# Retention and a gated feed-forward layer on one core: two transposes moved to TensorE, and other block widths behind the first 512 tokens

## The chip, the core and the metric

The kernel runs on one core of a Trainium2 chip. A core has a matrix engine (TensorE, PE in the profile), a vector engine (VectorE, DVE), a scalar engine (ScalarE, ACT), a general engine (GpSimd, POOL) and a sync engine (SyncE, SP), which here only issues transfers (DMAs). TensorE writes into PSUM, which VectorE and ScalarE read; everything else lies in SBUF. The metric is the device time of one execution in microseconds, as the median of several runs. Before the change it is 331.77 us over 8 runs (331.12 to 333.21).

## The reference

Eight batches of eight heads, 576 positions, head size 64. The first half is retention, a causal linear attention with a decay per head:

```python
scores = scale * np.matmul(q, k.transpose(0, 1, 3, 2))
gamma = 1.0 - 2.0 ** (-5.0 - np.arange(H, dtype=np.float32))
rel = pos[:, None] - pos[None, :]
Dmat = np.where(rel >= 0, gamma[:, None, None] ** rel[None, :, :], 0.0)
attn_out = np.matmul(scores * Dmat[None, :, :, :], v)
```

Its result is laid out as x with 4608 rows (tokens) of 512 columns, and the second half is a feed-forward layer with 1536 hidden columns:

```python
gate = 1.0 / (1.0 + np.exp(-(x @ w_gate)))
out = (gate * (x @ w_val)) @ w_out
```

## The kernel before, in words

The kernel works in bf16 with sums in float32. The decay is split into a factor on q and a factor on k, so that the scores only need a triangular mask.

**Attention.** The first 768 tokens (three pairs of 128-token chunks) are done in a start phase of their own. The rest are 30 steps, numbered 0 to 29 (`STEPS`), of 128 tokens and all heads each; step s fills columns 768 + 128 s of the transposed activations `xT` (the last two swapped). A step needs its q, k and v loaded (three transfers of 256 KB, `load`, L118), q and k scaled and cast to bf16 (`cast_qk`, L283, into `natural_qk`), v cast (L288), and a transposed copy `T` of q and k. The copy is made by `cross` (L290 to L294): one transposing DMA from SBUF to SBUF, issued by SP. `casts_to` (L590) puts loads, casts and transpose of a step into the program together, three steps ahead of the step's slot; steps 0 and 1 are put in before the blocks begin. SP takes everything in program order: the loads of step s+1 stand in front of the transpose of step s. GpSimd does most casts, also in program order; VectorE casts q of steps 0 and 1 and v of step 0.

On TensorE a step is a *slot* (`slot`, L511): the values of the step before (`intra` L493 with the masked scores, `inter` L507 with the running state), then the scores of this step (`scores`, L469, from `T`) and its state products (`products`, L477). VectorE then masks the scores (L484). The *after-phases* 0, 1 and 2 of a slot take the values out of PSUM: ScalarE casts one half of a value tile into `xT` (L526) and copies the shares that belong to the other tile (L529), VectorE adds the shares to the other half (L537), adds the state (L546, L550, L552), and ScalarE or GpSimd casts the state to bf16 (L446). The value tiles have one PSUM bank each (`VALS`: pools `pv_psum` and `tr_psum`), so the values of the next slot need all of these reads done. The score tiles have two banks (`qk_psum`).

**Feed-forward.** It goes by blocks of tokens. The first block, 512 tokens, is part of the start phase; its end is `op_first` (L888), with four output tiles stored by VectorE and ScalarE (L928 to L934). Behind it `BLOCKS` (L937) lists blocks of 256, 256, four of 384 and four of 512 columns. For each of the 12 chunks of hidden columns a block does four matmuls for the gate and four for the value (L625), a sigmoid on ScalarE and a product on VectorE. With 256 columns or fewer, gate and value share a PSUM bank and one unit of eight matmuls (L633 to L641); wider ones use a bank and a piece of four matmuls for each (L647 to L654). The banks of the units come from `ffn_psum`, which has three. Then come the output matmuls (`op_units`, L692), 12 for each 128 tokens, with a copy to SBUF on ScalarE (L668) and a store.

**The order.** Nothing is scheduled by a planner; the program order is what each engine runs. The loop over `BLOCKS` interleaves the two halves: `order` (L579) lists the phases ("slot", "after0", "after1", "after2" of each step), `end` is the last phase that the next block needs (the after-phases of the slot behind its last step), and after each unit or piece `advance` runs as many of the block's phases as its share of columns calls for:

```python
advance(begin + min(todo, -(-todo * max(0, gone - wait) // (total - wait - 3 * 2048))))
```

`gone` counts columns of matmul work done, `total` those of the block; 3 x 2048 columns at the end are left free. `wait`, 2048 columns, is set only for the block at token 512, so that slot 0 comes after its second unit.

Of the kernel before, what the change touches and what calls it, by code (L numbers as in the profile page):

```python
# [10 lines left out]
BF16 = mybir.dt.bfloat16  # L11
# [5 lines left out]
def kernel(  # L17
# [19 lines left out]
    nc = tc.nc  # L37

    B, H, S, D = q.shape
    NT, DM = out.shape  # L40
    DFF = moe_w_gate.shape[1]
    P = 128
    M = H // 2
# [7 lines left out]
    att_pool = ctx.enter_context(tc.tile_pool(name="att", bufs=3))  # L51
# [152 lines left out]
    ident = consts.tile([P, P], BF16)  # L204
# [41 lines left out]
    on_pool, on_act, on_dve = nc.gpsimd.tensor_copy, nc.scalar.copy, nc.vector.tensor_copy  # L246
# [8 lines left out]
    turned = {}  # L255
# [16 lines left out]
    natural_qk = {}  # L272
# [5 lines left out]
    def cast_qk(s, i, eng):  # L278
        c = STEPS[s][1]
        if i == 1:  # L280
            natural_qk[s] = nat_pool.tile([P, 2, M, P], BF16, tag="qk", name=f"qk_{s}")
        tab = (qtab, ktab)[i][:, c, :].rearrange("p (y m) -> p y m", y=2).unsqueeze(3).to_broadcast([P, 2, M, D])
        eng.tensor_tensor(out=natural_qk[s][:, i].rearrange("p m (y d) -> p y m d", y=2),  # L283
                          in0=by_halves(loaded[s][1 - i]), in1=tab, op=ALU.mult)

    def cast_v(s, eng):
        natural["v", s] = nat_pool.tile([P, H, D], BF16, tag="v", name=f"v_{s}")
        eng(out=natural["v", s], in_=loaded[s][2])  # L288

    def cross(s):  # L290
        t = att_pool.tile([P, 2, M, P], BF16, tag="T", name=f"T_{s}", bufs=5)
        nc.sync.dma_start_transpose(out=t.rearrange("p j m t -> p (j m) t"),
                                    in_=natural_qk[s].rearrange("p j m d -> p (j m d)"))
        turned[s] = t  # L294

    turned = {}
# [133 lines left out]
    def pair_out(A, a, *engs):  # L430
        t0 = (2 * A + a) * P
        k = M // len(engs)
        for i, eng in enumerate(engs):
            eng(out=xT[:, i * k:(i + 1) * k, t0:t0 + P], in_=pair_ps[2 * A + a][i * k][0])

    running = {}
    totals = {}

# [5 lines left out]
    def keep_state(key, src, eng):  # L444
        state[key] = new_state(key)
        eng(out=state[key], in_=src)  # L446
# [8 lines left out]
    VALS = [(pv_psum, "pv"), (tr_psum, "tr")]  # L455
# [55 lines left out]
    def slot(s):  # L511

        if s > 0:
            intra(s - 1)
            inter(s - 1)
        if s < NS:
            scores(s)
            if STEPS[s][1] < LAST:
                products(s)
        if s < NS:  # L520
            mask(s)
# [33 lines left out]
    def after(s, i):  # L555

        makes = s < NS and STEPS[s][1] < LAST
        to_bf16 = on_act if s < 6 else on_pool
        if i > 0 and s > 0:
            leave_other(s - 1, i - 1)  # L560
        if i < 2 and s > 0:
            leave_own(s - 1, i)
        if i < 2 and makes:
            add_state(s, i)
        if i > 0 and makes and (s, i - 1) in totals:
            b, c = STEPS[s]
            keep_state((b, c, i - 1), totals.pop((s, i - 1)), to_bf16)


    def first_batch_state():  # L570

        whole = new_state((0, LAST - 1, NJ - 1))
        for hh in range(2):
            for y in range(2):
                (nc.vector.tensor_copy if hh == y else nc.sync.dma_start)(
                    out=whole[half(y), hh::2, :], in_=sbd[3][half(hh), 2 * y:2 * y + 2, half(hh)])
        state[0, LAST - 1, NJ - 1] = whole

    order = []  # L579
    for s in range(NS + 1):  # L580
        order += [("slot", s), ("after0", s), ("after1", s), ("after2", s)]

    done = {"ld": 0, "cast": 0}

    def loads_to(s):
        while done["ld"] <= min(NS - 1, s):
            load(done["ld"])
            done["ld"] += 1

    def casts_to(s):  # L590
        while done["cast"] <= min(NS - 1, s):
            x = done["cast"]
            loads_to(x + (1 if x < 12 else 2))
            cast_qk(x, 1, nc.gpsimd)
            cast_qk(x, 0, nc.vector if x < 2 else nc.gpsimd)
            cross(x)
            cast_v(x, on_dve if x == 0 else on_pool)
            done["cast"] += 1

    def run_phase(kind, s):  # L600
        if kind == "slot":
            slot(s)
            if s == 3:
                first_batch_state()
            casts_to(s + LEAD_CAST)
        else:
            after(s, int(kind[5]))

# [51 lines left out]
    def leave():  # L660
        r, ob = stores.pop(0)
        for p0, r0, w in rows(r, P):
            nc.sync.dma_start(out[r0:r0 + w, :], ob[p0:p0 + w])

    def store(opp, r0, eng=None):

        ob = osb_pool.tile([P, DM], FP32, tag="osb", name=f"ob_{r0}")
        (eng or on_act)(out=ob, in_=opp)  # L668
        stores.append((r0, ob))
        if len(stores) > KEEP:  # L670
            leave()
# [27 lines left out]
    def ffn_units(t0, n):  # L699
        gvs = {}  # L700
        yield from h_units(gvs, range(NFC), t0, 0, n)
        yield from op_units(gvs, t0, n)
# [3 lines left out]
    def advance(end):  # L706
        nonlocal at
        while at < end:
            run_phase(*order[at])
            at += 1  # L710

    def upto(s):

        return order.index(("after2", s + 1)) + 1

    def last_step(t1):
        return max(s for s in range(NS) if at_col[s] < t1)
# [170 lines left out]
    def op_first(fcs, nbs, opps):  # L888
        for fc in fcs:
            for nb in nbs:  # L890
                nc.tensor.matmul(opps[nb], lhsT=gvs[fc][:, nb * P:(nb + 1) * P], rhs=wo_sb[:, fc, :],  # L891
                                 start=(fc == 0), stop=(fc == NFC - 1))
# [23 lines left out]
    keep_state((1, 0, 1), st_tiles[1], on_act)  # L916
    op_first((5, 6, 7, 8, 9), range(3), opps)
    casts_to(0)
    third_intra([PV, QK[0]])
    pair_st(2, 1)  # L920
# [4 lines left out]
    nc.vector.tensor_copy(out=running[1], in_=st_tiles[1])  # L925
    keep_state((1, 1, 1), running[1], on_act)
    op_first((10, 11), range(3), opps)
    store(opps[0], 0, on_dve)  # L928
    opps.append(qk_psum.tile([P, 512], FP32, tag="qk", name="op_0_3"))
    op_first(range(0, 6), (3,), opps)  # L930
# [2 lines left out]
    store(opps[2], 2 * P, on_dve)  # L933
    store(opps[3], 3 * P, on_act)  # L934
    casts_to(1)

    BLOCKS = [(512, 256), (768, 256)] + [(t, 384) for t in range(1024, 2560, 384)]  # L937
    BLOCKS += [(t, 512) for t in range(2560, NT, 512)]
    pieces = 0
    for w, (t0, n) in enumerate(BLOCKS):  # L940
        nxt = BLOCKS[w + 1] if w + 1 < len(BLOCKS) else None
        end = upto(last_step(nxt[0] + nxt[1])) if nxt else len(order)
        todo = end - at
        begin = at
        total = 2 * NFC * 4 * n + 12 * 512 * (n // P)
        gone = 0
        wait = 2048 if t0 == 512 else 0
        for cols in ffn_units(t0, n):
            gone += cols
            pieces += 1  # L950
            if stores and (nxt is None or w + 2 == len(BLOCKS) and pieces % 4 == 0):
                leave()
            advance(begin + min(todo, -(-todo * max(0, gone - wait) // (total - wait - 3 * 2048))))
        advance(end)
    while stores:
        leave()
# [29 lines left out]
```

## Time and profile before

| | |
|---|---|
| median of 8 runs | 331.77 us (331.12 to 333.21) |
| profiled execution, its own time | 331.83 us |
| its span in the profile | 330.1 us |
| granted TensorE clock | 1.00 of full speed |
| TensorE matmul / weight load busy | 321.1 / 181.0 us |
| VectorE / ScalarE / GpSimd busy | 154.4 / 131.1 / 117.0 us |
| block at token 512 | 52.59 to 72.04 us |
| block at token 768 | 72.04 to 90.29 us |
| from there to the block at token 2560 | 90.29 to about 193.6 us |
| transposing DMAs (`T`) | 30, median 4.7 us from issue to landing (3.0 to 6.3) |
| loads of k, q, v (256 KB each) | 26 of each, median 4.7, 5.2 and 5.5 us to landing |

The page gives the busy time of each engine, and then the costliest groups of instructions: line, engine, operation, tiles, how many, busy time and mean of one, and the idle time ahead of them with what ended it. Matmuls overlap in the pipeline, so a matmul's own duration is longer than the distance from one to the next, and it is the distance that counts. The timeline has one row for a run of equal instructions: start, duration, engine, line, operation, count, and in brackets the idle time before it and its releaser. The chain of waits is the work that ended last, followed back from the end.

### The profile page before, as it was taken

The page shows a single profiled execution, that of the slowest core. Times are in us where ns is not written, and L with a number is a line of the kernel's source. Part 1 is how long each engine was busy: PE and PEld are TensorE (multiplying, and loading weights), DVE is VectorE, ACT ScalarE, POOL GpSimd, SP SyncE. Part 2 cuts the span into 40 slices and gives each one's busy share as a digit, 9 for nine tenths or more (in the row PEclk, how much of TensorE's full clock was granted, in tenths as well). Part 3 has the DMA queues.
Part 4 walks back from the last instruction along what each step waited for, and adds up shares of the span by engine and source line. Part 5 has one row for each costly group of instructions (what it writes and reads, how often), then busy time and mean ns, then how long its engine had stood idle before and what let it go on. Part 6 is the DMA issues. An engine that isn't in the chain of part 4 may idle for free.

```text
span 330.1 us, 9167 instructions
## 1 busy us (share of the span) xinstructions
PE 321.1 (97%) x3749; PEld 181.0 (55%) x3776; DVE 154.4 (47%) x367; ACT 131.1 (40%) x332; POOL 117.0 (35%) x171
## 2 busy tenths in 40 slices
PE   8899999899999999999999999999999999999996
PEld 8764546758566456456556544444444444444443
DVE  5845536637446255246346625541555056204310
ACT  6655544445443244243343433432443233333321
POOL 5674543445364636115534536052444000000000
PEclk9999999999999999999999999999999999999999
DMA  8999999999999999996796998859314900020003
GB/s 220 306 363 352 339 278 198 188 189 165 196 203 177 178 243 177 236 222 133 202 149 129 204 239 175 122 143 211 65 32 115 326 11 0 3 95 32 2 33 95
DMA packets 146906, 55.68 MB, mean 169 GB/s; under 512 B 127280, under 2 KB 138800, under 8 KB 146864
## 3 DMA queue, kind: packets, MB, share of 16 engines
q1 hardware_dynamic: 146720, 54.97, 81.2%
q8 instruction: 29, 0.48, 0.6%
q10 hardware_dynamic: 144, 0.13, 0.1%
q14 instruction: 13, 0.11, 0.1%
HBM read 37.75 MB, written 9.44 MB: 143 GB/s over the span
## 4 chain that ended last, share of the span: by engine, by line
PE 79%; DMA 14%; SPq 4%; POOL 2%; issue 1%; ACT 0%
PE h L625 48%; PE op L692 24%; PE val L493 2%; SPq L130 2%; DMA wv<-in_moe_w_val_dram 2%; DMA k<-in_k_dram 2%; DMA T<-qk 2%; DMA k32p<-in_k_dram 2%; DMA v32p<-in_v_dram 2%; DMA v<-in_v_dram 2%; DMA wo<-in_moe_w_out_dram 2%; DMA wg<-in_moe_w_gate_dram 1%; PE row L477 1%; PE row L469 1%; PE val L507 1%
## 5 line engine op out<-in xcount | busy, mean ns | idle before, releaser
L625 PE MATMUL h<-xT,wv_sb 128*128 128x384 bf16 (+2 forms) x470 | 102.4, 336 | 0.5
L625 PE MATMUL h<-xT,wg_sb 128*128 128x384 bf16 (+2 forms) x479 | 102.8, 337 | 0.1
L653 DVE TENSOR_TENSOR gv<-g,h 128x384 bf16<-128x384 bf16 (+1 forms) x96 | 59.6, 621 | 61.1 <-PE h L625 54.1
L649 ACT ACTIVATE g<-h 128x384 bf16<-128x384 f32 (+1 forms) x96 | 52.2, 544 | 89.1 <-PE h L625 85.8
L692 PE MATMUL op<-wo_sb,gv 128*128 128x512 bf16 x361 | 81.3, 379 | 1.0 <-issue 0.6
L625 PEld LDWEIGHTS <-wg_sb 128*128 128x128 bf16 x480 | 46.2, 98 | 36.9
L625 PEld LDWEIGHTS <-wv_sb 128*128 128x128 bf16 x480 | 45.5, 98 | 33.6
L692 PEld LDWEIGHTS <-gv 128*128 128x128 bf16 x372 | 36.0, 98 | 42.3
L446 POOL CAST sb<-s 128x256 bf16<-128x256 f32 x35 | 14.0, 403 | 101.1 <-DVE s L550 66.3
L484 DVE TENSOR_TENSOR pt<-row,tri 128x256 bf16<-128x256 f32 x60 | 22.6, 419 | 53.1 <-PE row L477 47.3
L668 ACT COPY ob<-op 128x512 f32<-128x512 f32 x33 | 19.3, 586 | 61.8 <-PE op L692 58.3
L283 POOL TENSOR_TENSOR qk<-k,ktab 128x512 bf16<-128x512 f32 x30 | 31.3, 1044 | 25.4 <-DMA k<-in_k_dram 21.0
L283 POOL TENSOR_TENSOR qk<-q,qtab 128x512 bf16<-128x512 f32 x28 | 29.2, 1044 | 3.1 <-DMA q<-in_q_dram 2.4
L288 POOL CAST v<-v 128x512 bf16<-128x512 f32 x29 | 17.7, 612 | 9.2 <-DMA v<-in_v_dram 7.8
L537 DVE TENSOR_TENSOR xT<-val,share 128x128 bf16<-128x128 f32 x54 | 15.4, 285 | 11.7 <-ACT share L529 11.6
L529 ACT COPY share<-val 128x128 f32<-128x128 f32 x54 | 15.1, 280 | 5.6 <-DVE xT L537 4.7
L526 ACT CAST xT<-val 128x128 bf16<-128x128 f32 x60 | 15.6, 264 | 1.4 <-PE val L507 1.4
L550 DVE TENSOR_TENSOR s<-s,row 128x256 f32<-128x256 f32 x39 | 16.1, 412 | 0.0
L641 DVE TENSOR_TENSOR gv<-g,h 128x256 bf16<-128x256 bf16 x24 | 10.1, 420 | 12.6 <-ACT g L639 12.0
L639 ACT ACTIVATE g<-h 128x256 bf16<-128x256 f32 x24 | 9.1, 386 | 12.5 <-PE h L625 12.0
L493 PEld LDWEIGHTS <-v 64*64 64x64 bf16 x480 | 6.5, 107 | 11.5 <-issue 11.3
L891 PE MATMUL op<-wo_sb,gv 128*128 128x512 bf16 x45 | 11.2, 379 | 0.3 <-issue 0.2
(96 smaller groups left out, 243.3 us busy)
## 6 DMA issues: line engine op xcount, KB each, us to landing
out_dram<-ob SPq DMA_DIRECT2D x31, 256.0 KB, 2.4
k<-in_k_dram SPq DMA_DIRECT2D x26, 256.0 KB, 4.7
q<-in_q_dram SPq DMA_DIRECT2D x26, 256.0 KB, 5.2
v<-in_v_dram SPq DMA_DIRECT2D x26, 256.0 KB, 5.5
wg<-in_moe_w_gate_dram SPq DMA_DIRECT2D x12, 256.0 KB, 5.4
wv<-in_moe_w_val_dram SPq DMA_DIRECT2D x12, 256.0 KB, 5.3
wo<-in_moe_w_out_dram SPq DMA_DIRECT2D x12, 256.0 KB, 5.3
k32p<-in_k_dram SPq DMA_DIRECT2D x6, 256.0 KB, 5.6
```

What stands on the lines that cost most here:

```text
L283: eng.tensor_tensor(out=natural_qk[s][:, i].rearrange("p m (y d) -> p y m d", y=2), in0=by_halves(loaded[s][1 - i]), in1=tab, op=ALU.mult)
L288: eng(out=natural["v", s], in_=loaded[s][2])
L484: nc.vector.tensor_tensor(out=probs[s][:, y], in0=row_ps[s][y][:, 0], in1=tri.unsqueeze(1).to_broadcast([P, M, 64]), op=ALU.mult)
L526: nc.scalar.copy(out=xT[:, own, cols_of(s, j)], in_=val_ps[s][j][:, own])
L529: nc.scalar.copy(out=shares[s, j], in_=val_ps[s][1 - j][:, M:M + 2])
L537: nc.vector.tensor_tensor(out=xT[:, other, cols_of(s, j)], in0=val_ps[s][j][:, other], in1=shares.pop((s, j)), op=ALU.add)
L550: nc.vector.tensor_tensor(out=new, in0=running[b], in1=p, op=ALU.add)
L625: nc.tensor.matmul(out, lhsT=w_sb[:, kc, fc * P:(fc + 1) * P], rhs=xT[:, kc, t0 + a:t0 + e], start=(kc == 0), stop=(kc == NKC - 1))
L649: nc.scalar.activation(out=g[:, 0:n], in_=h1[:, 0:n], func=AF.Sigmoid)
L653: nc.vector.tensor_tensor(out=gvs[some[0]][:, a:e], in0=g[:, 0:n], in1=h2[:, 0:n], op=ALU.mult)
L668: (eng or on_act)(out=ob, in_=opp)
L692: nc.tensor.matmul(opp, lhsT=gvs[fc][:, nb * P:(nb + 1) * P], rhs=wo_sb[:, fc, :], start=(fc == 0), stop=(fc == NFC - 1))
```

## The change

A function `turn_step` makes the transposed copy of a step on TensorE: 8 transposes (a matmul with the identity) into the two banks of the value tiles, four in each, one bank copied out by ScalarE and one by VectorE. Steps 0 and 1 use it in place of the transposing DMA (`TURNED = 2`). Step 0 is turned between two groups of output matmuls of the first block; step 1 gets a phase of its own in `order`, between after-phases 1 and 2 of slot 0. The blocks behind the first 512 tokens become 256, 384, 384 and six of 512 columns, so ten blocks become nine, and which phases fall into which block changes with them. `wait` goes.

```diff
+    TURNED = 2
+
+    def turn_step(s):
+
+        t = att_pool.tile([P, 2, M, P], BF16, tag="T", name=f"T_{s}", bufs=5)
+        for i, ((pool, tag), eng) in enumerate(zip(VALS, (on_act, on_dve))):
+            ps = pool.tile([P, M, P], BF16, tag=tag, name=f"turn_{s}_{i}")
+            for m in range(M):
+                nc.tensor.matmul(ps[:, m, :], lhsT=natural_qk[s][:, i, m, :], rhs=ident, is_transpose=True,
+                                 start=(m == 0), stop=(m == M - 1))
+            eng(out=t[:, i], in_=ps)
+        turned[s] = t
...
-        order += [("slot", s), ("after0", s), ("after1", s), ("after2", s)]
+        order += [("slot", s), ("after0", s), ("after1", s)] + [("turn", s + 1)] * (s + 1 == 1) + [("after2", s)]
...
-            cross(x)
+            if x >= TURNED:
+                cross(x)
...
+        elif kind == "turn":
+            turn_step(s)
...
     op_first((10, 11), range(3), opps)
+    turn_step(0)
     store(opps[0], 0, on_dve)
...
-    BLOCKS = [(512, 256), (768, 256)] + [(t, 384) for t in range(1024, 2560, 384)]
-    BLOCKS += [(t, 512) for t in range(2560, NT, 512)]
+    BLOCKS = [(512, 256), (768, 384), (1152, 384)] + [(t, 512) for t in range(1536, NT, 512)]
...
-        wait = 2048 if t0 == 512 else 0
...
-            advance(begin + min(todo, -(-todo * max(0, gone - wait) // (total - wait - 3 * 2048))))
+            advance(begin + min(todo, -(-todo * gone // (total - 3 * 2048))))
```

In the changed kernel the lines behind `pair_out` stand 13 to 16 lines lower, so that L537 becomes L550 and L625 becomes L641.

## The prediction

> **What bounds the kernel now.** I read the page first, then the tensor engine's waits, then the timeline around its longest wait, then the chain of waits from 45 to 80 us. The page's busy times, and its shares of the chain that ended last:
>
> ```profile
> PE 321.1 (97%) x3749; PEld 181.0 (55%) x3776; DVE 154.4 (47%) x367; ACT 131.1 (40%) x332; POOL 117.0 (35%) x171
> ...
> PE 79%; DMA 14%; SPq 4%; POOL 2%; issue 1%; ACT 0%
> ```
>
> TensorE is busy 321.1 of 330.1 us. From 90.3 us on, the timeline shows attention slots and FFN pieces back to back, so only TensorE work counts there. What can be won lies between 50 and 85 us, where these waits are:
>
> ```profile
> PE val L493 <- DVE xT L537: 0.8, 1, 0.8
> ...
> PE row L469 <- DMA T<-qk: 0.3, 1, 0.3
> ```
>
> The longest one on TensorE's timeline (start, us, what):
>
> ```profile
> 63.45 0.60 PE L625 MATMUL h<-xT,wv_sb 128*128 128x256 bf16 x4
> 63.98 0.22 PE L493 MATMUL val<-pt,v 64*64 64x64 bf16 x2
> 65.04 0.31 PE L493 MATMUL val<-pt,v 64*64 64x64 bf16 x14 [0.84 <-DVE xT L537]
> 65.16 0.32 PE L507 MATMUL val<-T,sb 64*64 64x64 bf16 x16
> 65.60 0.32 PE L469 MATMUL row<-T 64*64 64x64 bf16 x16
> 65.75 0.30 PE L477 MATMUL row<-v,qk 64*64 64x64 bf16 x16
> 65.98 0.61 PE L625 MATMUL h<-xT,wg_sb 128*128 128x256 bf16 x4
> ```
>
> This is slot 2. It starts its values for step 1 and must wait until VectorE has taken step 0's values out of the same PSUM bank. Why VectorE is late is in ScalarE's and VectorE's own timelines:
>
> ```profile
> 62.40 0.38 ACT L639 ACTIVATE g<-h 128x256 bf16<-128x256 f32 x1 [0.49 <-PE h L625]
> 62.68 0.26 ACT L526 CAST xT<-val 128x128 bf16<-128x128 f32 x1
> 63.47 0.27 ACT L529 COPY share<-val 128x128 f32<-128x128 f32 x1 [0.53 <-DVE xT L537]
> 63.64 0.41 ACT L446 CAST sb<-s 128x256 bf16<-128x256 f32 x1
> 63.94 0.66 ACT L639 ACTIVATE g<-h 128x256 bf16<-128x256 f32 x2
> ```
>
> ```profile
> 63.16 0.28 DVE L537 TENSOR_TENSOR xT<-val,share 128x128 bf16<-128x128 f32 x1
> 63.36 0.41 DVE L546 TENSOR_TENSOR sf<-s,row 128x256 bf16<-128x256 f32 x1
> 64.36 0.42 DVE L641 TENSOR_TENSOR gv<-g,h 128x256 bf16<-128x256 bf16 x1 [0.60 <-ACT g L639]
> 64.70 0.28 DVE L537 TENSOR_TENSOR xT<-val,share 128x128 bf16<-128x128 f32 x1
> ```
>
> ScalarE's share (63.47) waits for VectorE's first xT; the next sigmoid, whose matmuls ended near 63.0, starts at 63.94; VectorE's product waits for it, and the second xT, which TensorE needs, stands behind that product. The transposed tile is not far off either:
>
> ```profile
> 59.23 6.33 DMA T<-qk
> 65.60 0.32 PE row L469 x16
> ```
>
> T_2 lands at 65.56, some 0.1 us after the rows could have started.
>
> **What the skill says.** "TensorE: Matmul & The Clock Gate", section "Architectural detail", has ScalarE and VectorE strictly first in, first out; the trace agrees, the sigmoid above stayed behind the share. "PSUM — Partial Sum Buffer", section on bank collisions, says that the two engines must be kept apart on one bank even for reads; the trace agrees, shares waited 4.7 us for xT, 8 times. The TensorE page's "Back-to-back issue gap" gives N/2.4 + 2.5 ns for N columns; pieces of four follow here at 0.437, 0.650 and 0.864 us, which is 109.3, 162.5 and 215.9 ns a matmul, so it holds. Its "Part 4: PE-mode transpose" gives about 275 ns for a transpose in a kernel; the trace has four in a row (39.00 to 39.23 us) costing 0.23 us, so I use 57 ns.
>
> **The change, part by part.**
>
> *Blocks.* 10 blocks become 9, so 96 matmuls and weight loads of h go while their columns stay. Columns 512 to 2560 before: 192 at 109.3 + 384 at 162.5 = 83.39 us. After: 96 at 109.3 + 192 at 162.5 + 192 at 215.9 = 83.15 us. Gain 0.24 us. Weight loads (98 ns) fit under even the 109 ns matmul.
>
> *Transposes on TensorE.* Two turns of 8 transposes, 16 x 57 ns = 0.92 us, all on TensorE's busy path, plus about 0.06 us because turn 0's second half needs the bank that VectorE's copy L403 leaves at 50.44: cost 0.97. Each turn also adds a ScalarE copy (0.59 to 0.74 us, row L320) and a VectorE copy (none from bf16 PSUM is in the trace; between 0.42 us, a half-size copy, and 0.69, a PSUM copy of this shape; I take 0.68). For turn 0 they go ahead of the stores of the first 512 rows: ScalarE then ends the store of op_0_3 near 53.95, just when slot 0 needs that bank. For turn 1 they run from about 57.0 to 58.0, before slot 1 at 58.4. I count both at nothing; if that cover fails, each costs up to 0.6. The buffers of T_0 and T_1 come free to T_5 and T_6 only after these copies and slots 1 and 2, long before those transposes are issued (77.9 and 83.5 before).
>
> *Transposes off SP and DMA.* Two issues leave SP (2.94 and 2.43 us). Slot 0 waited for T_0: it took 0.79 us (54.34 to 55.13) where I put a free one at 0.5, gain 0.3. Slot 1 took 0.87 against 0.75 for a free full slot (later ones take 0.69 to 0.79): gain 0.12. T_2 comes earlier: from 54.7 (T_0) to 76.9 (T_4, k_6 lands one load later) four steps took 5.55 us each; at about 1.2 us a load (k_2 landed 55.96, one load after T_0) a transpose is worth some 1.9 us, two of them 3.8. T_2 so lands near 61.7 and T_3 near 67.3, estimates good to about 1 us.
>
> *Order of attention in block 512.* This decides. The next block is now 384 wide, so 17 phases (slots 0 to 3, their after-phases, the turn) instead of 12 go into the 512-token block, and the initial wait of 2048 columns is gone. After unit i (12 h units, 2048 columns each) the count reached is 17*2048*i/30720 rounded up (36864 columns of the block less 3 x 2048): 2, 3, 4, 5, 6, 7, 8, 10, 11, 12, 13, 14. So slot 0 comes after unit 1, turn 1 after 3, slot 1 after 5, and after unit 8 both the last after-phase of slot 1 and slot 2: nothing lies between them. Before, one unit lay between (units 10 and 11). Slot 3 follows unit 12, its predecessor's last phase unit 11.
>
> Follow it with 0.875 us a unit, from 53.1 (52.59 + 0.5): unit 5 ends 58.43, slot 1 59.18, units 6, 7, 8 end 60.05, 60.93, 61.80. A sigmoid starts 0.25 after its unit and takes 0.38; a product follows and takes 0.42. Sigmoid 7 61.18, product 7 61.60, first xT ends 62.22, share to 62.52, the state cast to 62.83, so sigmoid 8 starts at 62.72 (engines overlap by some 0.1), product 8 63.14, second xT ends 63.76, TensorE resumes at 63.82. With the 0.94 us from resumption to the next piece, as before, slot 2 ends at 64.76, against 62.55 if free: 2.2 us lost. Before it lost 2.09 - 0.75 = 1.34. Loss +0.86. T_2's rows come about 64.2, so T_2 is in time.
>
> The same walk for slot 3: unit 12 ends 68.26, the second xT ends 69.34, the slot ends 70.34, 1.33 lost (as slot 2 before, same spacing). Before, slot 3 stood behind the output matmuls and took 0.69, nothing lost. Loss +1.33. T_3's rows come near 69.8, about 2.5 us after my estimate. SP and GpSimd keep their order past slot 3; its two small state DMAs and 0.77 us of VectorE copies now fall into the output stage, where VectorE idled from 69 to 73.6.
>
> *Blocks behind.* Slots 4 and 5 took 0.95 and 0.93 us among 256-column units. In 384-column pieces they have two pieces behind the last after-phase, as slots 7 to 18 of before, which show no such wait: gain 0.4. Slots 7 to 14 come up to 6 us earlier; supply of 5.6 us a step stays ahead of their 6 to 7.5.
>
> *Sum:* -0.24 + 0.97 - 0.30 - 0.12 + 0.86 + 1.33 - 0.40 = +2.1 us on a span of 330.1. The profiled execution's time is 331.83, 1.7 above its span, and the median is 331.77; the same margin gives 333.9.
>
> **Rivals.**
>
> *The transposes are late (12%).* T_3 now is needed near 69.8 instead of 73.3. For: T landed up to 6.3 us after issue, with DMA share 1.2 to 1.5 from 50 to 75 us. Against: two transposes fewer. If loads ahead of it keep today's pace (T_3 at 71.7 before: k_5, one load behind it, lands at 72.9), it holds slot 3 by about 1.9 more: 335.8. It decides from a landing after 69.8.
>
> *The waits are hidden, faster (13%).* If xT of slot 1 and 2 leaves PSUM before slots 2 and 3 arrive, their losses are 0 and before's 1.34 is won too: +0.97 - 0.24 - 0.3 - 0.12 - 1.34 - 0.4 = -1.4, so 330.4. For: the wait is only 2 to 3 short operations. Against: product 8 cannot start before unit 8 has ended, which alone (0.25 + 0.38 + 0.42 + 0.28) holds slot 2 for 1.3 us. It decides if TensorE resumes there within 0.3 us.
>
> *About a wash (9%).* The chain is short at both places (1.3 at slot 2, 0.5 at slot 3, including the slower restart): 2.1 - 0.9 - 0.8 = +0.4, 332.2. It would need ScalarE to take each sigmoid as soon as its unit ends.
>
> **Numbers.** My case has 66%, with its own range 332.8 to 335.0 (slot 2 losing only 1.3 + 0.2 of restart, or both copies uncovered). The 8-in-10 range takes in the wash and nearly all of late T_3, not the faster case: 331.3 to 335.8. This kernel can tell 0.2%, 0.66 us, from no change. Slower: 66 + 12 + 1 (the upper edge of the wash) = 79%; same 8%; faster 13%.
>
> **What would show it.** Slot 2 and slot 3 each with an idle of TensorE put down to VectorE's xT (now L550), about 1.9 and 1.1 us; no wait for T at slots 0 to 3; T_2 landing 61 to 63; four transposes at 0.23 us; 864 h matmuls in L641; the block of 768 starting near 75.5. I am wrong if TensorE runs through slot 2, or if a wait for T or for ScalarE's stores appears before 70 us.

## The result and the profile after

The changed kernel takes 335.06 us (median of 11 runs, 333.73 to 337.2), the kernel before 331.77 us beside it (median of 32): a ratio of 1.010, 95% interval 1.0074 to 1.0126. It is slower, as forecast, by 3.3 us where 2.1 were forecast. The profiled execution took 334.12 us over a span of 332.4 us, which is 2.3 us more than before's and 0.2 us above the forecast sum. Of the 11 and the profiled one, seven ran at a granted clock of 1.000 and took 333.73 to 335.06 us (median 334.12), five at 0.990 to 0.995 and took 335.82 to 337.2, so the median holds about another microsecond that the trace does not show.

The same rows of the page as before, the busy times and the shares of the chain that ended last:

```profile
PE 321.1 (97%) x3664; PEld 172.3 (52%) x3696; DVE 155.4 (47%) x357; ACT 130.4 (39%) x322; POOL 117.2 (35%) x171
...
PE 82%; DMA 10%; SPq 4%; issue 1%; DVE 1%; ACT 1%; POOL 0%; ACTq 0%
```

TensorE's busy time is the same 321.1 us. It has 80 weight loads fewer: 96 of h are gone, as the same columns go in fewer instructions, and the 16 transposes are new. By this page, on which the ends of matmuls are modelled, the 2.3 us are idle time of TensorE. VectorE and ScalarE have entered the last chain with 1% each. The waits of TensorE that are new or larger (total us, times, longest):

```profile
PE val L506 <- DVE xT L550: 1.9, 2, 1.0
...
PE val L506 <- ACT share L542: 0.6, 1, 0.6
...
PE turn L444 <- DVE apart L403: 0.2, 1, 0.2
```

The wait for a transposed tile, 0.3 us before, is gone. On TensorE's timeline (start, us, what) slots 2 and 3 look like this:

```profile
61.69 0.60 PE L641 MATMUL h<-xT,wv_sb 128*128 128x256 bf16 x4
62.90 0.22 PE L506 MATMUL val<-pt,v 64*64 64x64 bf16 x2 [0.61 <-ACT share L542]
64.15 0.31 PE L506 MATMUL val<-pt,v 64*64 64x64 bf16 x14 [1.03 <-DVE xT L550]
...
64.80 0.61 PE L641 MATMUL h<-xT,wg_sb 128*128 128x256 bf16 x4
...
68.40 0.22 PE L506 MATMUL val<-pt,v 64*64 64x64 bf16 x2
69.46 0.31 PE L506 MATMUL val<-pt,v 64*64 64x64 bf16 x14 [0.84 <-DVE xT L550]
...
70.06 5.35 PE L708 MATMUL op<-wo_sb,gv 128*128 128x512 bf16 x23
```

Slot 2 goes from the end of the unit at 62.13 to 64.80: 2.67 us where it took 2.09. Slot 3 goes from 68.31 to 70.06: 1.75 us where it took 0.69. ScalarE's and VectorE's timelines in front of slot 2's resumption:

```profile
61.51 0.38 ACT L655 ACTIVATE g<-h 128x256 bf16<-128x256 f32 x1 [0.16 <-PE h L641]
...
62.59 0.27 ACT L542 COPY share<-val 128x128 f32<-128x128 f32 x1 [0.53 <-DVE xT L550]
62.75 0.41 ACT L459 CAST sb<-s 128x256 bf16<-128x256 f32 x1
63.05 0.39 ACT L655 ACTIVATE g<-h 128x256 bf16<-128x256 f32 x1
```

```profile
62.27 0.28 DVE L550 TENSOR_TENSOR xT<-val,share 128x128 bf16<-128x128 f32 x1
62.47 0.41 DVE L559 TENSOR_TENSOR sf<-s,row 128x256 bf16<-128x256 f32 x1
63.48 0.42 DVE L657 TENSOR_TENSOR gv<-g,h 128x256 bf16<-128x256 bf16 x1 [0.59 <-ACT g L655]
63.81 0.28 DVE L550 TENSOR_TENSOR xT<-val,share 128x128 bf16<-128x128 f32 x1
```

It is the walk of the prediction, piece by piece: share behind the first xT, state cast, sigmoid 8 at 63.05, product 8 at 63.48, second xT at 63.81, TensorE at 64.15. Each piece comes 0.3 us later than in the walk, as the block began at 53.41 and not at 53.1. One wait more than forecast is seen: TensorE's first two value matmuls stood 0.61 us for ScalarE's share, an earlier link of the same chain. The last part of the chain of waits is:

```profile
62.75 0.41 ACT sb L459
63.16 0.29 ACT g L655
...
63.48 0.42 DVE gv L657
63.90 0.21 DVE xT L550
...
64.15 0.31 PE val L506 x14
```

The other place is the first turn. Its second half waits for VectorE's copy out of the bank:

```profile
50.01 0.39 PE L444 MATMUL turn<-ident,qk 128*128 128x128 bf16 x4
50.60 0.38 PE L444 MATMUL turn<-ident,qk 128*128 128x128 bf16 x4 [0.21 <-DVE apart L403]
50.83 2.75 PE L907 MATMUL op<-wo_sb,gv 128*128 128x512 bf16 x12
```

From 50.01 to 50.83 are 0.82 us for 8 transposes, and by as much block 512 starts later (53.41 after 52.59). The second turn, beside h units, costs 0.44.

### The profile page after: what moved, and what is told of

Its sections match the earlier page's. It is cut to its first block, busy times and chain, and to the rows that moved or that the text cites. A ratio compares the mean times of both kernels' runs of the same rounds, so it can differ in the third digit from the quotient of the medians.

```text
span 332.4 us, 8969 instructions
## 1 busy us (share of the span) xinstructions
PE 321.1 (97%) x3664; PEld 172.3 (52%) x3696; DVE 155.4 (47%) x357; ACT 130.4 (39%) x322; POOL 117.2 (35%) x171
## 4 chain that ended last, share of the span: by engine, by line
PE 82%; DMA 10%; SPq 4%; issue 1%; DVE 1%; ACT 1%; POOL 0%; ACTq 0%
PE h L641 50%; PE op L708 24%; DMA wv<-in_moe_w_val_dram 3%; SPq L130 3%; PE val L506 2%; DMA v<-in_v_dram 2%; DMA wg<-in_moe_w_gate_dram 2%; DMA k32p<-in_k_dram 2%; PE row L490 1%; PE row L482 1%; DMA wo<-in_moe_w_out_dram 1%; PE val L520 1%; PE op L697 1%; PE op L907 1%; SPq L142 1%
## 5 line engine op out<-in xcount | busy, mean ns | idle before, releaser
L641 PE MATMUL h<-xT,wv_sb 128*128 128x512 bf16 (+2 forms) x416 | 100.0, 355 | 0.8
L641 PE MATMUL h<-xT,wg_sb 128*128 128x512 bf16 (+2 forms) x431 | 100.6, 355 | 0.1
L669 DVE TENSOR_TENSOR gv<-g,h 128x512 bf16<-128x512 bf16 (+1 forms) x96 | 62.8, 655 | 65.2 <-PE h L641 61.2
L665 ACT ACTIVATE g<-h 128x512 bf16<-128x512 f32 (+1 forms) x96 | 54.8, 571 | 96.3 <-PE h L641 95.3
L641 PEld LDWEIGHTS <-wg_sb 128*128 128x128 bf16 x432 | 41.9, 98 | 41.1
L641 PEld LDWEIGHTS <-wv_sb 128*128 128x128 bf16 x432 | 40.6, 98 | 37.5 <-issue 0.2
L684 ACT COPY ob<-op 128x512 f32<-128x512 f32 x33 | 19.4, 587 | 62.9 <-PE op L708 56.2
L550 DVE TENSOR_TENSOR xT<-val,share 128x128 bf16<-128x128 f32 x54 | 15.4, 285 | 10.9 <-ACT share L542 10.9
L506 PE MATMUL val<-pt,v 64*64 64x64 bf16 x480 | 10.0, 198 | 2.5 <-DVE xT L550 1.9
L334 DVE TENSOR_TENSOR ptp<-qkp,trip 128x512 bf16<-128x512 f32 x12 | 7.6, 683 | 4.4 <-PE qkp L329 4.3
```

The source lines that it names most:

```text
L506: nc.tensor.matmul(val_ps[s][j][half(x), kc, :], lhsT=natural["v", s][half(j), h, :], rhs=probs[s][half(j), h // M, h % M, :], start=(kc = ...
L550: nc.vector.tensor_tensor(out=xT[:, other, cols_of(s, j)], in0=val_ps[s][j][:, other], in1=shares.pop((s, j)), op=ALU.add)
L641: nc.tensor.matmul(out, lhsT=w_sb[:, kc, fc * P:(fc + 1) * P], rhs=xT[:, kc, t0 + a:t0 + e], start=(kc == 0), stop=(kc == NKC - 1))
L665: nc.scalar.activation(out=g[:, 0:n], in_=h1[:, 0:n], func=AF.Sigmoid)
L669: nc.vector.tensor_tensor(out=gvs[some[0]][:, a:e], in0=g[:, 0:n], in1=h2[:, 0:n], op=ALU.mult)
```

## The experiments

They ran in four groups, each on one chip and beside the kernel before. The start phase differs from execution to execution (arrival of loads, in two runs the granted clock), so block 512 starts anywhere from 52.6 to 56.5 us; blocks only, without any turn, starts where the changed kernel does. What a change does inside the block is therefore read from its length, start of its first h matmul to that of block 768. "Rest" is from there to the end of the last matmul. Among the waits, g stands for a sigmoid and gv for a product. All in us, from the timeline of one execution of each run; the ratio is to the kernel before on the same chip.

| run | start of 512 | its length | rest | waits of TensorE in it | ratio, 95% |
|---|---|---|---|---|---|
| before | 52.59 | 19.45 | 254.85 | xT 0.84, T 0.26 | |
| after | 53.41 | 21.84 | 253.86 | xT and share 2.48 | 1.0100 (1.0074 to 1.0126) |
| turns only | 53.21 | 19.16 | 254.93 | xT 0.84 | 1.0015 (0.9997 to 1.0034) |
| blocks only | 53.41 | 24.26 | 253.74 | T 3.23, xT 1.68 | 1.0134 (1.0116 to 1.0153) |
| after, phases apart | 53.48 | 21.18 | 253.87 | xT 1.69 | 1.0034 (0.9997 to 1.0071) |
| after, phases first | 53.88 | 21.81 | 253.84 | xT 0.84, T 0.53, gv 0.84 | 1.0048 (1.0030 to 1.0065) |
| after again | 54.41 | 21.84 | 253.76 | xT and share 2.48 | 1.0086 (1.0050 to 1.0121) |
| before, grouped | 54.39 | 17.97 | 255.38 | none | 1.0018 (1.0001 to 1.0035) |
| after, grouped | 56.51 | 19.55 | 254.57 | g 0.60 | 1.0062 (1.0035 to 1.0089) |
| after, grouped, turn late | 53.47 | 21.56 | 254.51 | T 1.72, g 0.61 | 1.0052 (1.0024 to 1.0079) |
| before, first three grouped | 52.81 | 19.82 | 254.92 | T 1.76 | 0.9987 (0.9967 to 1.0008) |
| after, first three grouped, turn late | 52.90 | 21.82 | 253.81 | T 1.98, g 0.60 | 1.0048 (1.0026 to 1.0069) |
| turns only, first three grouped, turn late | 52.89 | 18.14 | 254.67 | none | 0.9966 (0.9950 to 0.9983) |
| after, the same, four turns | 52.77 | 20.31 | 253.78 | none | 0.9999 (0.9974 to 1.0024) |

The changed block list puts slot 3 into block 512, which is why its rest is about a slot shorter.

**One half of the change at a time.** Turns only is the changed kernel with the block list and the `wait` of the kernel before:

```diff
-    BLOCKS = [(512, 256), (768, 384), (1152, 384)] + [(t, 512) for t in range(1536, NT, 512)]
+    BLOCKS = [(512, 256), (768, 256)] + [(t, 384) for t in range(1024, 2560, 384)]
+    BLOCKS += [(t, 512) for t in range(2560, NT, 512)]
...
+        wait = 2048 if t0 == 512 else 0
...
-            advance(begin + min(todo, -(-todo * gone // (total - 3 * 2048))))
+            advance(begin + min(todo, -(-todo * max(0, gone - wait) // (total - wait - 3 * 2048))))
```

> The two turns on TensorE, with the blocks and the free first unit of the kernel before. Theory (order of the phases costs, the turns only cost their own TensorE time): +0.82 us for turn 0 with its wait for VectorE's copy, +0.44 for turn 1, -0.31 at slot 0, -0.1 each at slots 1 and 2 where T was waited for; slot 2 still waits about 0.85 us for VectorE. Span +0.7 to +0.9 us against before. Rival (the landing of the transposes held slots 0 to 2, and VectorE's wait only hid it): slot 2's wait goes, span -0.5 us or better.

Measured: span 330.6, which is 0.5 us over before's, less than expected (the first turn took 0.63 us here); ratio 1.0015; slot 2 kept its 0.84 us wait for xT. The turns win the T wait back and nothing else. Blocks only has the new list and no turns (`TURNED = 0`, no turn phase):

> The new blocks and no free first unit, but every transpose by DMA. Theory: T_0 to T_3 land as in the kernel before (about 54.7, 59.1, 65.5, 71.7 us) and slots 0 to 3 come sooner, so each waits for its T by 1 to 2 us; the block at 768 starts near 77.5 us and the span is 334 to 335 us, some 2 us over the full change. Rival (the turns are pure cost, the transposes would have been in time): span about 1.2 us under the full change, near 331.2.

Measured: span 334.6, and block 768 at 77.67, as expected. Without the turns, all four slots of the block wait for their transposed tile (1.40, 0.83, 0.47 and 0.53 us, three of them under the 1 to 2 us expected) on top of the two xT waits of 0.84 us. So the loss is in the block list and its order; the turns are worth 2.4 us of block length beside it (24.26 to 21.84), and in the old order they bring no gain in time (1.0015).

**The spacing of the phases.** Two edits of the changed kernel:

```diff
-            advance(begin + min(todo, -(-todo * gone // (total - 3 * 2048))))
+            advance(begin + min(todo, -(-todo * gone // (total - (2 if t0 == 512 else 3) * 2048))))
```

> The full change with 2 x 2048 instead of 3 x 2048 columns left free at the end of the block at 512: one unit then lies between the last after-phase of slot 1 and slot 2, and slot 3 moves behind the first four output matmuls. Theory: slot 2's waits fall from 1.64 us to the 0.85 to 1.05 of the kernel before, slot 3 keeps about 1 us; span -0.6 us against the full change. Rival (slot 2 waits because ScalarE and VectorE are behind in this block as a whole, not because of the spacing): no change in span.

Measured: 0.66 us off the block and 0.6 off the span, as expected. With one unit between the last after-phase and slot 2, the wait is the 0.84 us of the kernel before in place of 1.64; slot 3 keeps 0.85. The ratio, 1.0034, is further below the changed kernel's than 0.6 us makes; the trace does not show why.

In the second edit, a unit of gate and value yields ahead of its sigmoid, so that phases are issued before it:

```diff
-                    if i < len(some) - 1:
-                        yield 8 * n
+                    yield 8 * n
...
-                yield 8 * n
             else:
```

> The full change, but in 256-column units the phases are put into the program after the unit's matmuls and ahead of its sigmoid and product. Theory (first in, first out: the value copies stand behind the newest product): the waits at slots 2 and 3 fall to under 0.2 us each, slot 2 takes about 0.8 instead of 2.67 us and slot 3 about 0.75 instead of 1.75; span -2.5 to -2.9 us against the full change, so about 0.5 us under the kernel before. Rival (ScalarE and VectorE have too much to do there in any order, the more with the turns' copies): the waits move by less than half and the span stays above the kernel before.

It missed: the span is 332.8 us and the block keeps its length, 21.81. One xT wait fell to 0.84 and one went, but T of step 3 came up behind it (0.53), and the output matmuls got a wait of their own. From VectorE's and TensorE's timelines of this run:

```profile
70.28 2.09 DVE L588 COPY sf<-sbd 64x128 bf16<-64x128 bf16 x2
72.40 0.42 DVE L656 TENSOR_TENSOR gv<-g,h 128x256 bf16<-128x256 bf16 x1
```

```profile
72.88 1.47 PE L706 MATMUL op<-wo_sb,gv 128*128 128x512 bf16 x6 [0.84 <-DVE gv L656]
```

The last product of the block had been put behind slot 3's mask and the two state copies. Those copies took 2.09 us here and 0.38 in other runs (see the last section), so this wait hangs on the execution, and the one profiled was the slowest of seven; the ratio of 1.0048 lies below the changed kernel's 1.0100 and 1.0086. The two edits shift this stall and may shorten it; neither removes it.

**The evacuation itself.** The wait is built from two engines that alternate on two banks: ScalarE reads bank 0, VectorE bank 0, ScalarE's share bank 0 again, VectorE bank 1, with a sigmoid and a product between them. The regrouping lets ScalarE read all it needs of one bank in one phase, and puts both of VectorE's additions behind that in after-phase 1:

```diff
-        nc.scalar.copy(out=xT[:, own, cols_of(s, j)], in_=val_ps[s][j][:, own])
-        if before(s, j) is not None:
...
-            nc.scalar.copy(out=shares[s, j], in_=val_ps[s][1 - j][:, M:M + 2])
+        if before(s, 1 - j) is not None:
...
+            nc.scalar.copy(out=shares[s, 1 - j], in_=val_ps[s][j][:, M:M + 2])
+        nc.scalar.copy(out=xT[:, own, cols_of(s, j)], in_=val_ps[s][j][:, own])
...
-        if i > 0 and s > 0:
-            leave_other(s - 1, i - 1)
         if i < 2 and s > 0:
             leave_own(s - 1, i)
+        if i == 1 and s > 0:
+            leave_other(s - 1, 1)
+            leave_other(s - 1, 0)
```

> The kernel before, with the evacuation of the slots' value banks regrouped: ScalarE reads one bank at a time (own half and the share kept in that bank), and both of VectorE's additions follow in the second phase after the slot instead of the second and the third, so that whole units of h matmuls lie between them and the next slot. Theory (the stall of slot 2 is the alternation of ScalarE and VectorE on the two banks, standing behind sigmoid and product in their queues): the 0.84 us wait of slot 2 for xT and its restart go, slot 2 falls from 2.09 us to about 0.8 to 1.0, the span from 330.1 to 328.8 to 329.2 us. Rival (the stall only moves to the h matmuls or to the next slot, since ScalarE and VectorE have the same work to do): span within 0.3 us of 330.1.

> The changed kernel with the same regrouping. Theory: slot 2 falls from 2.67 to about 0.8 us and slot 3 from 1.75 to about 0.8 us, nothing takes their place, and the span falls from 332.4 by 2.3 to 2.8 us, to 329.6 to 330.1 us: then the loss of the change is this evacuation chain and nothing else of weight. Rival (the denser phases leave too little time for ScalarE and VectorE in any order): one of the two waits stays or a new one appears in the output matmuls, as when the phases were put ahead of the sigmoid, and the gain is under 1.3 us.

In both the block shrank as the theory says, by 1.48 us (17.97) and by 2.29 (19.55), and in both the time did not follow: 1.0018 and 1.0062, with spans of 331.0 and 333.9 us, above what was expected. Both profiled executions had run part of the start phase at a lower clock (0.88 and 0.86 from 10 to 20 us), with runs of four 256-column matmuls at 1.04 us there instead of 0.61, and started block 512 1.8 and 3.1 us late: their transposed tiles were ready by then. Only 4 of 22 and 1 of 12 executions had a mean clock under 0.998, so these two traces are not typical. The next run shows an ordinary start. It also moves the first turn and the state copies:

```diff
     op_first((10, 11), range(3), opps)
-    turn_step(0)
...
     op_first(range(0, 6), (3,), opps)
+    turn_step(0)
...
-            if s == 3:
+            if s == 6:
                 first_batch_state()
```

> The changed kernel regrouped, with the first turn put behind the first six output matmuls of row block 3 and the two state copies on VectorE moved from slot 3 to slot 6. Theory: the wait of the first turn for VectorE's copy of the third pair (0.21 to 0.36 us) goes and the rest is as in the run with the regrouping alone: 0.2 to 0.4 us less span than that one. Rival (the turn of step 0 costs its matmuls wherever it stands, and its wait hides another): within 0.1 us of it.

The late turn works: 0.44 us and no wait. But the block is 21.56 us long, and TensorE's timeline says why:

```profile
62.95 0.32 PE L506 MATMUL val<-pt,v 64*64 64x64 bf16 x16 [0.61 <-ACT g L656]
...
63.88 0.32 PE L482 MATMUL row<-T 64*64 64x64 bf16 x16 [0.49 <-DMA T<-qk]
...
69.47 0.32 PE L482 MATMUL row<-T 64*64 64x64 bf16 x16 [1.23 <-DMA T<-qk]
```

No xT wait is left, and the transposes of steps 2 and 3, issued by SP at 57.91 and 63.19 and in place some 6 us later, take their place. Whatever brings slots 2 and 3 forward runs into them. All three runs with every step regrouped also have a longer rest, by 0.5 to 0.8 us. In the grouped kernel of the old list ScalarE's sigmoids wait more for VectorE (19.4 us in 16 waits, 2.2 in 3 before) and some pieces of h take 0.79 us in place of 0.65; that the one makes the other was not tried apart. The regrouping was therefore kept to the dense block. The repetition of the changed kernel:

> The changed kernel again, unaltered, beside the others on one chip. If the part of its median that the trace does not show (3.3 us over the kernel before, of which 2.3 us are in the profiled execution) is chance in the granted clock of the executions that were drawn, the median falls to 2.2 to 2.6 us over the kernel before; if it belongs to the change, it stays at 3 us or more.

Measured: 335.07 against 332.57, 2.5 us, and in the trace the same three waits, 2.48 us. Executions with a granted clock of at least 0.998 alone have a median of 334.33 (6) against 332.05 (31), 2.3 us.

**Both together.** The regrouping for steps 0 to 2 alone, in the kernel before, in turns only, and in the changed kernel; the last two with the late turn, and all with the state copies at slot 3:

```diff
-        if i > 0 and s > 0:
+        if i > 0 and s > NEAR:
             leave_other(s - 1, i - 1)
         if i < 2 and s > 0:
             leave_own(s - 1, i)
+        if i == 1 and 0 < s <= NEAR:
+            leave_other(s - 1, 1)
+            leave_other(s - 1, 0)
```

`NEAR` is 3, and `leave_own` goes by banks only for s < NEAR.

> The kernel before with the evacuation of steps 0 to 2 regrouped and no turn. Theory: T of step 2, landing at about 65.5 us by the clock of the transfers, takes the place of the xT wait at slot 2; the stretch of block 512 shrinks by 0.2 to 0.5 us where its start is at 52.6 us as in the kernel before, with a wait for T at slot 2 in the trace, and the time is within 0.15% of before. The later blocks, which the regrouping of all steps made 0.5 us longer, keep the length they have in the kernel before. Rival (the transfer is no bound): a full 1.1 to 1.3 us less, ratio about 0.9965.

> The block sizes of before with the two turns, the first of them behind six of the output matmuls of row block 3, and the evacuation of steps 0 to 2 alone regrouped by banks. Theory (two waits stood at slot 2 of the kernel before, one behind the other: xT until 65.0 us, and T of step 2, which comes from SP's queue at 65.5 us; the turns move SP's order for step 2 from 59.2 to 57.7 us, the regrouping removes the xT wait, and only both together pay): the stretch from the start of block 512 to that of block 768 is 17.9 to 18.3 us where the kernel before has 19.45 and the turns alone 19.16; with 0.44 us for the first turn the span is 0.5 to 0.9 us under that of before, ratio 0.997 to 0.9985. Rival (the two together give what each gave alone, and the turns' matmuls eat it): ratio 1.000 or above.

> The changed kernel with the first turn late and the evacuation of steps 0 to 2 alone regrouped. Theory: as in the run that regrouped all steps, T of steps 2 and 3 takes the place of the xT waits (0.5 and 1.2 us there), so that block 512 stays at 21 to 21.6 us; the later blocks are 0.4 us shorter than there: span 332.2 to 332.5 at an undisturbed clock, ratio to before 1.004 to 1.0055. Rival (the new block sizes lose only by the evacuation chain): ratio below 1.002.

In the kernel before, T takes over at slot 2, as its timeline shows:

```profile
65.15 0.30 PE L507 MATMUL val<-T,sb 64*64 64x64 bf16 x16
66.19 0.32 PE L469 MATMUL row<-T 64*64 64x64 bf16 x16 [0.74 <-DMA T<-qk]
```

Its time stays within the measurement of before (0.9987). Its block did not shrink in the execution profiled, against the 0.2 to 0.5 us expected: T of steps 0 and 1 was late too, by 0.72 and 0.30 us. With turns and regrouping together nothing waits:

```profile
64.30 0.32 PE L506 MATMUL val<-pt,v 64*64 64x64 bf16 x16
...
64.57 0.30 PE L482 MATMUL row<-T 64*64 64x64 bf16 x16
```

Block 512 is 18.14 us, as expected, the rest 254.67, the span 329.0 and the median 331.03 us against 332.43: faster than both kernels, by 0.34% (0.17 to 0.50%) over the one before. Neither part had been faster alone beyond its interval (1.0015 and 0.9987). Times alone do not show that the two bring more together than their sum: this run also has the late turn, which turns only has not (0.45 us for the first turn in place of 0.63), and the intervals are about 0.2% wide to each side. The traces show why they should: at slot 2 the xT wait and the late T stand one behind the other, turns only leaves the first and the regrouping alone leaves the second.

In the changed kernel, the third run, T waits of 0.73 and 1.25 us, and 0.60 for a sigmoid, hold the block at 21.82. The last run gives it turns for steps 2 and 3 too, both halves into one bank of `ffn_psum` and one VectorE copy:

```diff
-    TURNED = 2
+    TURNED = 4
...
+        if s >= 2:
+            ps = ffn_psum.tile([P, 2, M, P], BF16, tag="ffn", name=f"turn_{s}")
...
+            on_dve(out=t, in_=ps)
...
-        order += [("slot", s), ("after0", s), ("after1", s)] + [("turn", s + 1)] * (s + 1 == 1) + [("after2", s)]
+        order += [("slot", s), ("after0", s), ("after1", s)] + [("turn", s + 1)] * (s + 1 < TURNED) + [("after2", s)]
```

> The changed kernel as in the run with the evacuation of steps 0 to 2 regrouped and the first turn late, and steps 2 and 3 transposed on TensorE as well (both halves into one of the h units' banks, one copy by VectorE). Theory (with the xT waits gone, the transfers of T of steps 2 and 3 are what holds the new first block): the waits for T at slots 2 and 3 (0.73 and 1.25 us) go, the two turns cost 0.88 us, block 512 falls from 21.82 to 20.5 to 21.1 us and the ratio to before from 1.0048 to 1.000 to 1.0035. Rival (ScalarE and VectorE are full there, and a VectorE copy of each turn puts the stall back before slots 2 and 3): no gain, ratio 1.0045 or more.

Measured: no wait of TensorE in the block, 20.31 us (below the range expected), ratio 0.9999 (0.9974 to 1.0024). So with its stalls out the changed kernel comes level with the kernel before, which has its own; its span is 1.0 us above that of the best run, of which its two more turns make 0.9 (0.45 us each).

## Why the prediction was right, and where its terms were off

- **Direction and mechanism held.** Slower, because slots 2 and 3 come right behind the after-phases and wait for xT behind a sigmoid and a product. The chain of waits passes through exactly those instructions, and the regrouping removes the xT waits by changing only the order in that chain. The 0.61 us for the share is part of it; the prediction had the whole loss as waits for xT.
- **The terms beside what they came to.** Slot 0: -0.31 (forecast -0.30). Slot 1: -0.08 (-0.12). Slots 4 and 5: from 0.95 and 0.93 to 0.79 and 0.83, -0.26 (-0.40). Transposes: 0.82 + 0.44 = 1.26 (0.97). Slot 2: +0.58 (+0.86). Slot 3: +1.06 (+1.33). With -0.24 for the blocks, which was not measured apart, they add up to +2.0 of the 2.3 us; where the remaining 0.3 lies was not traced. Errors of 0.3 with both signs cancelled in the sum: that it came within 0.2 us of the span is in part luck.
- **The restart was over-priced.** I took 0.94 us from resumption to the next piece from slot 2 of before. That number had T of step 2 in it: the rows came 0.44 us behind the state's part of the values there (L507, 65.16 to 65.60), and come 0.12 behind it (L520) at 64.28 to 64.40. Without it the restart is 0.65 and 0.60 us. I had written that T landed some 0.1 us after the rows could have started, where these distances make it 0.3, and still used the sum as the price of a restart.
- **The first turn was under-priced.** I gave its second half 0.06 us of waiting for VectorE's copy. TensorE was ready at 50.24 (50.01 and four transposes), the copy ended at 50.55, 0.1 us later than before, and the second half began at 50.60: 0.36 us. Putting the turn six matmuls later (the late turn) makes it 0.44 us.
- **VectorE's copy of a turned tile** took 0.42 us, the lower end of what I allowed; nothing waited for it.
- **The transposes landed 2 us later than forecast.** T_2 landed at 63.67 and T_3 at 69.52 (6.0 and 6.3 us after their issues), where I had 61.7 and 67.3:

```profile
57.69 2.06 SPq L292 DMA_TRANSPOSE T<-qk  x1
...
63.23 2.33 SPq L292 DMA_TRANSPOSE T<-qk  x1
```

  Two transposes fewer brought each forward by 1.9 and 2.0 us, not by 3.8. They had held SP's queue for 5.37 us; but the six loads issued next to them, which held it for 3.9 us before, now hold it for 7.5; why they take longer is open. I had also read T_4's landing before as 76.9; it is 75.97.
- **The transposes being late** was a rival at 12%, and it did not happen, but by little: the rows of step 2 started at 64.40 and those of step 3 at 69.64, 0.1 us after T_3 landed. Of the 2.5 us to spare that I forecast for T_3, its late landing used up 2.2, so that it held nothing up was luck. Slot 3 was itself held by xT until 69.46; in the runs where the xT waits are gone, T takes 1.7 to 2.0 us back. So "the waits are hidden, faster" would have been wrong about the time even if the evacuation had been quick, because I had worked it out with no wait for T behind it.
- **The price of a matmul** held. The formula that the prediction quotes from the Trainium skill, "TensorE: Matmul & The Clock Gate", section "Back-to-back issue gap", is given there for a matmul by itself; that matmuls in a stream keep to it is what this trace shows (109.3, 162.5 and 215.9 ns).
- **The median's other microsecond** was not forecast. In the repetition the difference at full clock is 2.3 us, as in the traces; in the first measurement the clocks of the kernel before are not on record. Executions under a granted clock of 0.998 are 12 of 43 of the kernel before and 10 of 23 of the changed one; whether the change makes them more frequent is open.

## What to carry to other kernels

A stall can cover a second one just behind it: before pricing the removal of a wait, look at what the next instruction would have waited for at that time, and price a restart from a place without such a second wait. Two remedies that each measure as nothing may still pay together when each leaves the other's wait standing, as the traces of the turns and the regrouping show here. Where two engines empty shared banks in turn, letting each take all it needs of one bank at once removed the waits in the dense block; the three runs that had the same regrouping everywhere were 0.5 to 0.8 us longer behind it.

## What was not expected of the hardware

The two small state copies at slot 3 (SBUF to SBUF, 64x128 bf16) took 0.38 us together in six of the runs, 0.77 before, 1.93 in the changed kernel (1.44 in its repetition) and 2.09 in the run with phases first. From the timeline of the changed kernel, GpSimd and VectorE:

```profile
70.67 1.04 POOL L283 TENSOR_TENSOR qk<-k,ktab 128x512 bf16<-128x512 f32 x1 [2.84 <-DMA k<-in_k_dram]
70.88 1.93 DVE L588 COPY sf<-sbd 64x128 bf16<-64x128 bf16 x2
71.71 1.04 POOL L283 TENSOR_TENSOR qk<-q,qtab 128x512 bf16<-128x512 f32 x1
```

The copies end at 72.81, just after GpSimd's second cast at 72.75. With phases first it is 72.37 and 72.32. In the changed kernel with the first three grouped, where both copies took 0.38 us, they started at 70.32, ahead of GpSimd's cast at 70.51. The Trainium skill, "SBUF — State Buffer", section "Who interferes with whom", says that a VectorE copy in a two-port mode and a GpSimd instruction exclude each other for a whole instruction; the times agree, at up to 1.7 us (2.09 less 0.38), though no trace shows the mode of a copy. The copies were covered by output matmuls in the changed kernel, and were not with phases first.

VectorE's copy of a bf16 tile out of PSUM took 0.416 us for 512 columns and 0.684 for 1024 (in the run with four turns), so 0.52 ns a column. Of float32 tiles it took 0.418 us for 256 columns and 0.680 for 512, so 1.02. "VectorE: DVE Perf Modes", section "The perf-mode tier table", allows a copy from PSUM up to twice the plain rate; the traces agree, and I could have sized the term by that instead of taking a copy of float32.
